# A gated-linear-attention and expert kernel: fill transfers spread over the loads, weights and an expert choice moved later in the order

## The chip, the cores and the metric

The kernel runs on one core of a Trainium2 chip. Its time is the device time of one execution in microseconds (us); smaller is better. Runs of one kernel are compared by their median. TensorE (PE) does the matmuls, VectorE (DVE), ScalarE (ACT) and GpSimd (POOL) the element work; SyncE (SP) issues most transfers. Each engine works through its own list of instructions in order.

## What is computed

A recurrence over 768 steps for 4 batches and 8 heads of width 48, and behind it a mixture of 16 experts in 4 groups. Each of the 3072 rows goes through the one expert that its two argmaxes pick:

```python
for t in range(S):
    state = alpha[:, :, t, :, None] * state + np.einsum('bhd,bhe->bhde', k[:, :, t], v[:, :, t])
    y[:, :, t] = np.einsum('bhd,bhde->bhe', q[:, :, t], state)
...
g_logits = x @ w_group
g_idx = np.argmax(g_logits, axis=1)
...
e_logits = xg @ w_expert[g]
e_idx = np.argmax(e_logits, axis=1)
...
h = np.maximum(xg[mask_e] @ w1[g, e], 0.0)
ye = h @ w2[g, e]
out[tok_idx] = combined[:, None] * ye
```

## The kernel before

**Chunks.** The recurrence is done in 24 chunks of 128 steps (six for each batch). For chunk n, DVE runs two scans over the decays (`rev`, line 445, and `forth`, line 456, with a small reciprocal `turn` between them), POOL multiplies keys and queries by their results (`key`, line 461, and `query`, line 465), and PE makes, in this order: the scores of chunk n+1 (`score`, line 477), its keys turned (`turn_k`, line 506), the rows of chunk n-1 with their logits (`row`, line 565), the gain of the state (`gain`, line 519), the outputs (`own_out`, line 543), and what the state adds (`from`, line 552). The scores are masked either by one DVE multiplication (line 486) or by an ACT copy (line 491) and a POOL select (line 494), once for each of the two halves of the heads; `BY_VECTOR[n]` says how many of chunk n's two halves DVE takes. The next chunk's scores go to the same PSUM banks, so `score` of n+1 waits for both masks of n. DVE adds the gain to the state (`grow`, line 528), ACT scales it in four pieces (`scale`, line 532) and copies the outputs (`copy`, line 558).

**Transfers.** A chunk's input is one array of 128 rows of 1925 numbers: decays, keys, queries, values. Chunks 0 and 1 come in pieces, the others whole. They land in six buffers (`in`), chunks 6 to 9 in the buffers of expert weights (`w`). All go through SP's list, with a few of the first ones through ACT's. Between them stand eight `fill` transfers, which write blank rows over the first 224 places of all 16 experts in the scratch tensor `slots_d` (line 777), and the weights of expert 0 (`w1`, `w2`). A fill needs the tile `blank`, which POOL makes (lines 243 and 244). Transfers signal on eight semaphores in turn, so at most eight are under way, and an issue waits until the one eight places earlier has landed.

**Experts.** After each batch (three smaller groups in the last batch) the experts of the rows are chosen, their places counted, and the rows scattered to `slots_d` by POOL (line 716). Expert 0 starts early with 96 rows. When three batches are counted, DVE chooses the expert with the most rows so far (`choose_ahead`, lines 328 to 338, step `ahead`), and SP loads its weights first (`w11`, `w21`). Then all experts run, with PE reading two weight matrices of 1.5 MB for each (line 271).

**The order** is not the one of the code. A planner, `Plan`, holds every step with its engine, an estimated duration and what it comes after; it walks through an imagined time, each engine taking the ready step with the longest way to the end, and the steps are emitted in the order that results. So a change of a dependency or of an estimate can move steps that the edit does not name. Tiles and semaphores see to correctness whatever the order.

## Time and profile before

| | us |
|---|---|
| median of 3 runs | 400.14 (399.95 to 401.26) |
| the profiled execution, whole | 400.82 |
| its span in the profile | 399.1 |
| first score of a chunk on PE | 8.54 |
| score of chunk 9, chunk 10 | 46.73, 60.06 |
| score of chunk 22, chunk 23 | 114.62, 121.33 |
| first matmul of the chosen expert | 144.11 |
| last matmul of the experts | about 388 |

The profile gives starts and durations in us from the start of the span. A note such as `[1.57 <-DMA w<-in_rows_dram]` behind a row says that the engine sat idle for so long just before, and what ended it. PEclk is the clock granted to PE, 1.00 being full speed.

### The profile page before, as it was taken

How to read it: one execution, taken by the hardware profiler on the slowest of the kernel's cores; microseconds unless marked ns; L12 is line 12 of the kernel's file. 1: busy time of each engine (PE TensorE's matmuls, PEld its weight loads, DVE VectorE, ACT ScalarE, POOL GpSimd, SP SyncE). 2: the span in 40 equal slices, each digit the busy share in tenths (PEclk: the TensorE clock that was granted, in tenths of full speed). 3: DMA queues.
4: the chain of work that ended last, by engine and by line, in shares of the span. 5: the costliest groups of instructions: out<-in, count | busy, mean ns of one | idle time of the engine just before them, and what ended most of it. 6: DMA issues, size and time to landing. Idle time of an engine off the chain costs nothing.

```text
span 399.1 us, 8686 instructions
## 1 busy us (share of the span) xinstructions
PE 379.2 (95%) x3381; PEld 362.3 (91%) x3381; DVE 160.8 (40%) x352; ACT 116.9 (29%) x307; POOL 199.0 (50%) x229
## 2 busy tenths in 40 slices
PE   7999669999999979999999999999999999999994
PEld 5888558888878979999999999999999999999993
DVE  6994578889987620202193021120220220220210
ACT  1576336675744211112121111211211211211120
POOL 4985847899964420234161442624534514424443
PEclk9999969999989989999999999999999999999998
DMA  8999992996657289776586765866868768666400
GB/s 306 399 395 379 400 414 83 369 339 227 224 199 270 108 255 256 290 213 214 190 266 236 247 208 192 278 243 214 235 252 265 224 243 284 208 266 237 179 21 31
DMA packets 30810, 98.35 MB, mean 246 GB/s; under 512 B 17989, under 2 KB 18371, under 8 KB 26416
## 3 DMA queue, kind: packets, MB, share of 16 engines
q1 hardware_dynamic: 24736, 86.88, 62.9%
q0 software_dynamic: 4832, 9.55, 7.1%
q10 hardware_dynamic: 1200, 1.36, 1.1%
q8 instruction: 27, 0.44, 0.5%
q14 instruction: 15, 0.12, 0.1%
HBM read 82.61 MB, written 15.60 MB: 246 GB/s over the span
## 4 chain that ended last, share of the span: by engine, by line
PE 83%; DVE 6%; DMA 5%; issue 2%; POOL 1%; ACT 0%; DVEq 0%; POOLq 0%
PE bank L271 61%; DMA in<-in_rows_dram 5%; PE bank L565 5%; PE zs L477 4%; PE zo L543 4%; PE zs L271 3%; PE bank L519 2%; PE zo L552 2%; DVE kd L445 2%; PE zo L506 2%; DVE cq L456 1%; POOL out_dram L1125 1%; DVE sm L486 1%; DVE cnt L323 1%; POOL in L465 0%
## 5 line engine op out<-in xcount | busy, mean ns | idle before, releaser
L1125 POOL DMA_INDIRECT out_dram<-yq,dst_q x101 | 98.1, 972 | 157.0 <-DVE yq L1121 109.5
L271 PE MATMUL bank<-hT,w 128*128 128x216 f32 (+14 forms) x720 | 120.8, 328 | 0.0
L271 PEld LDWEIGHTS bank<-hT,w 128*128 128x128 f32 x720 | 118.7, 190 | 0.0
L271 PE MATMUL bank<-xt_e,w 128*128 128x213 f32 (+14 forms) x720 | 117.4, 323 | 0.0
L271 PEld LDWEIGHTS bank<-xt_e,w 128*128 128x128 f32 x720 | 115.5, 190 | 0.0
L1142 DVE CAST dst_q<-xq 128x7 int32<-128x7 f32 (+1 forms) x14 | 2.4, 172 | 161.2 <-DMA out_dram<-yq,dst_q 161.2
L286 ACT ACTIVATE hT<-bank 128x432 f32<-128x432 f32 (+15 forms) x64 | 31.2, 488 | 98.7 <-PE bank L271 98.7
L302 ACT COPY yT<-bank 128x432 f32<-128x432 f32 (+29 forms) x30 | 12.1, 402 | 104.4 <-PE bank L271 104.4
L716 POOL DMA_INDIRECT slots_d<-xr,place x24 | 24.0, 1000 | 16.0 <-issue 8.5
L445 DVE TENSOR_TENSOR_SCAN kd<-in,starts 112x516 f32<-112x516 f32 x20 | 24.4, 1220 | 8.9 <-DMA in<-in_rows_dram 6.0
L565 PE MATMUL bank<-wr,yt 112*128 112x116 f32 x192 | 27.7, 290 | 0.2 <-ACT yt L558 0.2
L461 POOL TENSOR_TENSOR in<-in,kd 112x512 f32<-112x512 f32 x20 | 23.7, 1183 | 7.6 <-DVE kd L445 6.5
L477 PE MATMUL zs<-in 48*128 48x128 f32 x320 | 23.7, 284 | 3.0 <-POOL in L465 2.0
L465 POOL TENSOR_TENSOR in<-in,cq 112x512 f32<-112x512 f32 x20 | 23.6, 1181 | 5.4 <-PE bank L565 3.2
L565 PEld LDWEIGHTS bank<-wr,yt 112*128 112x128 f32 x192 | 25.0, 203 | 0.9 <-ACT yt L558 0.4
L477 PEld LDWEIGHTS zs<-in 48*128 48x128 f32 x320 | 19.7, 187 | 6.7 <-issue 3.3
L456 DVE TENSOR_TENSOR_SCAN cq<-in,starts 112x516 f32<-112x516 f32 x20 | 24.6, 1229 | 1.6
L1118 DVE STREAM_TRANSPOSE yq<-yT 128x672 f32<-128x672 f32 (+2 forms) x16 | 12.9, 807 | 27.5 <-ACT yT L302 27.5
L543 PE MATMUL zo<-sm,in 128*64 128x128 f32 (+1 forms) x320 | 23.1, 277 | 0.1
L532 ACT ACTIVATE state<-sums,kd 112x48 f32<-112x48 f32 x64 | 17.9, 330 | 10.6 <-DVE sums L528 10.6
L543 PEld LDWEIGHTS zo<-sm,in 128*48 128x48 f32 (+1 forms) x320 | 19.0, 132 | 0.7 <-POOL in L461 0.2
L558 ACT COPY yt<-zo 112x512 f32<-112x512 f32 x24 | 14.0, 585 | 15.6 <-PE zo L552 14.3
(152 smaller groups left out, 350.0 us busy)
## 6 DMA issues: line engine op xcount, KB each, us to landing
w<-in_w_dram SPq DMA_DIRECT2D x34, 1536.0 KB, 7.3
in<-in_rows_dram SPq DMA_DIRECT2D x18, 962.5 KB, 10.9
slots_d<-blank SPq DMA_DIRECT2D x8, 686.0 KB, 17.4
w<-in_rows_dram SPq DMA_DIRECT2D x4, 962.5 KB, 15.8
xq<-slots_d SPq DMA_DIRECT2D x28, 85.8 KB, 6.7
xq<-slots_d SPq DMA_DIRECT2D x28, 73.5 KB, 6.2
out_dram<-yq,dst_q POOLq DMA_INDIRECT x101, 5.5
in<-in_rows_dram ACTq DMA_DIRECT2D x2, 256.0 KB, 7.3
```

Of the source, the lines that this page charges most:

```text
L271: nc.tensor.matmul(z, lhsT=w, rhs=x, start=first, stop=last, skip_group_check=True)
L286: nc.scalar.activation(out=hT[:, f0:f0 + 2, 0:n], in_=z[:, 0:2 * n].rearrange("p (f t) -> p f t", f=2), func=AF.Relu)
L445: nc.vector.tensor_tensor_scan(out=flat(c.kd[:, p0:p1])[:, ::-1], data0=c.t[0:R, A1 * p1:A1 * p0:-1], data1=one_col.to_broadcast([R, A1 * ...
L456: nc.vector.tensor_tensor_scan(out=flat(c.cq[:, p0:p1]), data0=c.t[0:R, A1 * p0:A1 * p1], data1=starts[0:R, A1 * p0:A1 * p1], initial=1.0, ...
L461: nc.gpsimd.tensor_tensor(out=c.k[:, p0:p1], in0=c.k[:, p0:p1], in1=c.kd[:, p0:p1, 1:A1], op=ALU.mult)
L465: nc.gpsimd.tensor_tensor(out=c.q[:, p0:p1], in0=c.q[:, p0:p1], in1=c.cq[:, p0:p1, 1:A1], op=ALU.mult)
L477: nc.tensor.matmul(c.zs[i][:, p, :], lhsT=c.k[r, p, :], rhs=c.q[r, p, :], start=True, stop=True)
L532: nc.scalar.activation(out=c.st[:, p, 0:D], in_=chunks[c.n - 1].sums[:, p], func=AF.Copy, scale=c.kd[:, p, 0:1])
L543: nc.tensor.matmul(of(c.zo, p)[o], lhsT=c.v[:, h * D:h * D + o.stop - o.start], rhs=c.sm[:, i, p, :], start=(p < 2), stop=(c.bc == 0), ski ...
L565: nc.tensor.matmul(z[:, p * W:(p + 1) * W], lhsT=c.yt[:, p, :], rhs=wr[:, p, :], start=True, stop=True)
L716: sent = nc.gpsimd.indirect_dma_start(out=slots_by[t], out_offset=bass.IndirectOffsetOnAxis(ap=m["place"][:, c:c + 1], axis=0), in_=xr[:, ...
L1125: nc.gpsimd.indirect_dma_start(out=out_by.popleft().rearrange("n (j w) -> (n j) w", j=4), out_offset=bass.IndirectOffsetOnAxis(ap=dst[:, b ...
```

## The change

It has five parts, and the planner makes of them one new order.

1. The eight fills no longer stand in pairs before loads 8, 9, 10 and 11, but before loads 7, 8, 9 (two), 10, 11, 12 and 13. The first weights of expert 0 move from before load 15 to before load 16. The planner is also told that chunk 16 and later wait for the chunk six back, not ten.
2. ACT gets a one-column copy as its first step, which brings its table load to the front of its list.
3. Chunk 2 is sent in three pieces (decays, keys and queries, values); first pieces are dealt to SP and ACT in another way.
4. `choose_ahead` also comes after the places and the weights of its group, and has a smaller lead.
5. `BY_VECTOR` gives DVE 19 mask halves where it had 24.

```diff
+        def first_function():
+            nc.scalar.copy(out=zeros[:, 0:1], in_=nothing[:, 0:1])
...
-        BY_VECTOR = [0, 2, 1, 1, 1, 0, 1, 1, 0, 0, 1, 2, 0, 2, 0, 1, 0, 2, 2, 0, 1, 2, 2, 2]
+        BY_VECTOR = [0, 0, 0, 1, 1, 2, 1, 0, 1, 0, 1, 2, 0, 2, 1, 0, 0, 2, 2, 0, 1, 1, 0, 1]
...
         begin("decay0", False, 0, 0, AW)
-        begin("key_0", True, 0, AW, KQ)
-        begin("query_0", False, 0, KQ, VW)
-        begin("decay1", True, 1, 0, AW)
-        begin("key_1", False, 1, AW, KQ)
-        begin("query_1", True, 1, KQ, VW)
-        begin("load2", False, 2)
+        begin("key_0", False, 0, AW, KQ)
+        add("table", ACT, 1.5, first_function, row="act", after=["nothing"])
+        begin("query_0", True, 0, KQ, VW)
+        begin("decay1", False, 1, 0, AW)
+        begin("key_1", True, 1, AW, KQ)
+        begin("query_1", False, 1, KQ, VW)
+        begin("decay2", True, 2, 0, AW)
+        begin("key_2", False, 2, AW, VW)
         begin("value0", True, 0, VW, IW)
-        begin("load3", False, 3)
-        begin("value1", True, 1, VW, IW)
+        begin("value1", False, 1, VW, IW)
+        begin("load3", True, 3)
+        begin("value2", False, 2, VW, IW)
...
-        for i in range(FILLS):
-            before_load(8 + i // 2, ("fill", i))
-        for k, item in ((15, ("w1", 0)), (17, ("w2", 0))):
+        for i, k in enumerate((7, 8, 9, 9, 10, 11, 12, 13)):
+            before_load(k, ("fill", i))
+        for k, item in ((16, ("w1", 0)), (17, ("w2", 0))):
             before_load(k, item)
...
-                o = n - LATER
+                o = n - (LATER if n < LATER + NIN else NIN)
...
-            add("ahead", DVE, 1.1, choose_ahead, after=[f"count{AHEAD_T - 1}"], lead=20.0)
+            add("ahead", DVE, 1.1, choose_ahead,
+                after=[f"count{AHEAD_T - 1}", f"place{g}", made["weighed", g]], lead=8.0)
```

Three places of the new order matter below. PE's own order is the same as before.

**SP, the loads with the fills between them.** Before, from load 6 (`w_215`) on; `w` are chunks 6 to 9, the first `in` is chunk 10, and `slots_d<-blank` is a fill:

```order
L439 DMA w_215<-in_rows_dram 128x1925
L439 DMA w_248<-in_rows_dram 128x1925
L777 DMA slots_d<-blank 112x2x784 x2
L439 DMA w_354<-in_rows_dram 128x1925
L777 DMA slots_d<-blank 112x2x784 x2
L439 DMA w_452<-in_rows_dram 128x1925
L777 DMA slots_d<-blank 112x2x784 x2
L439 DMA in<-in_rows_dram 128x1925
L777 DMA slots_d<-blank 112x2x784 x2
L439 DMA in<-in_rows_dram 128x1925 x4
```

Now, from load 7 (`w_347`) on, one fill standing ahead of these rows:

```order
L442 DMA w_347<-in_rows_dram 128x1925
L780 DMA slots_d<-blank 112x2x784
L442 DMA w_415<-in_rows_dram 128x1925
L780 DMA slots_d<-blank 112x2x784 x2
L442 DMA w_510<-in_rows_dram 128x1925
L780 DMA slots_d<-blank 112x2x784
L442 DMA in<-in_rows_dram 128x1925
L780 DMA slots_d<-blank 112x2x784
L442 DMA in<-in_rows_dram 128x1925
L780 DMA slots_d<-blank 112x2x784
L442 DMA in<-in_rows_dram 128x1925
L780 DMA slots_d<-blank 112x2x784
```

Up to load 9 the same bytes stand ahead as before; ahead of load 10 stand five fills where six stood, ahead of load 11 six where eight stood.

**DVE, chunks 10 and 11.** Before, from the first scan of chunk 10 (`kd_668`) on; `kd_741` is the first scan of chunk 11, `sums_770` the `grow` of chunk 7:

```order
L445 SCALAR_TENSOR_TENSOR kd_668<-in_550,starts_114 112x516
L451 RECIPROCAL starts_114<-kd_668 112x4
L585 TENSOR_REDUCE lg_117<-lgp_121 128x120
L456 SCALAR_TENSOR_TENSOR cq_669<-in_550,starts_114 112x516
L445 SCALAR_TENSOR_TENSOR kd_741<-in_644,starts_114 112x516
L410 COPY starts_114<-desc_f_78 128x4
L411 COPY starts_114<-floor_f_79 128x1
L528 TENSOR_TENSOR sums_770<-state1_116,bank_747 112x192
```

Now, from the first scan of chunk 10 (`kd_678`); `sm_732` is a mask half of chunk 8, `sums_769` the `grow` of chunk 7:

```order
L448 SCALAR_TENSOR_TENSOR kd_678<-in_581,starts_114 112x516
L454 RECIPROCAL starts_114<-kd_678 112x4
L459 SCALAR_TENSOR_TENSOR cq_679<-in_581,starts_114 112x516
L588 TENSOR_REDUCE lg_117<-lgp_121 128x120
L489 TENSOR_TENSOR sm_732<-zs0_708,causal_68 128x512
L413 COPY starts_114<-desc_f_78 128x4
L414 COPY starts_114<-floor_f_79 128x1
L634 TENSOR_REDUCE starts_114<-lg_117 128x30
L531 TENSOR_TENSOR sums_769<-state1_116,bank_750 112x192
```

The `grow` of chunk 7 stood behind the first scan of chunk 11; now it stands ahead of it, behind the second scan of chunk 10, and a mask of chunk 8 has come to DVE. On ACT the copy of chunk 7's outputs, which stood behind the first `scale` piece that this `grow` feeds, stands behind the third.

**DVE, the choice of the expert.** Before, the last rows of `choose_ahead` (four more of its rows and the `own` of the group stand ahead), the group's weights and places, and the two masks of chunk 21:

```order
L336 TENSOR_TENSOR key_ahead_1702<-is_ahead_92,tile_f_76 128x15
L338 TENSOR_REDUCE ahead_i_93<-key_ahead_1702 128x1
L663 TENSOR_REDUCE sums_e_1730<-dl_1660 128x30
L665 SCALAR_TENSOR_TENSOR es_1732<-sums_e_1730,starts_114 128x24
L667 TENSOR_REDUCE starts_114<-es_1732 128x6
L668 SCALAR_TENSOR_TENSOR starts_114<-sums_e_1730,starts_114 128x6
L700 TENSOR_REDUCE place_1749<-own_1698 128x6
L670 RECIPROCAL xr_84<-starts_114 128x24
L486 TENSOR_TENSOR sm_1761<-zs0_1688,causal_68 128x512
L486 TENSOR_TENSOR sm_1761<-zs1_1689,causal_68 128x512
L451 RECIPROCAL starts_114<-kd_1671 112x4
```

Now, from the group's `own` to the first row of `choose_ahead` (`cnt18`):

```order
L696 TENSOR_TENSOR own_1702<-bank_1681,picked_81 128x96
L666 TENSOR_REDUCE sums_e_1707<-dl_1665 128x30
L668 SCALAR_TENSOR_TENSOR es_1713<-sums_e_1707,starts_114 128x24
L670 TENSOR_REDUCE starts_114<-es_1713 128x6
L671 SCALAR_TENSOR_TENSOR starts_114<-sums_e_1707,starts_114 128x6
L703 TENSOR_REDUCE place_1724<-own_1702 128x6
L673 RECIPROCAL xr_84<-starts_114 128x24
L489 TENSOR_TENSOR sm_1735<-zs0_1692,causal_68 128x512
L454 RECIPROCAL starts_114<-kd_1676 112x4
L459 SCALAR_TENSOR_TENSOR cq_1677<-in_1548,starts_114 112x516
L531 TENSOR_TENSOR sums_1762<-state0_115,bank_1739 112x192
L323 TENSOR_TENSOR cnt18_1774<-seen_83 128x16
```

The six rows of the choice have gone from ahead of the weights, places and masks to behind the second scan of chunk 23 and the `grow` of chunk 20. One of the two masks of chunk 21 has gone to ACT and POOL. ACT's register load of the chosen expert has gone from behind the turned keys of chunk 21 to behind the rows of chunk 22.

## The prediction

> **What bounds the kernel now.** I read the busy table first, then the stretches of the program, then PE's waits, then the chain that ended last.

> ```profile
> PE 379.2 (95%) x3381; PEld 362.3 (91%) x3381; DVE 160.8 (40%) x352; ACT 116.9 (29%) x307; POOL 199.0 (50%) x229
> ```

> PE is the bound over the whole span. Whether that holds in each stretch is seen from the window table (columns: window, its length, busy us and instructions of PE, PE weight load, DVE, ACT and POOL, then PEclk, DMA share, GB/s):

> ```profile
> 47.90:60.10 12.20, 6.48 (x71) 5.83 (x71) 8.40 (x19) 4.09 (x11) 6.70 (x9) 0.72 1.00 415
> 60.10:94.40 34.30, 34.30 (x553) 30.11 (x554) 29.74 (x57) 22.90 (x70) 29.50 (x32) 1.00 0.71 259
> ...
> 113.70:121.40 7.70, 6.74 (x82) 5.86 (x78) 6.04 (x15) 3.13 (x11) 6.00 (x6) 0.78 0.88 334
> ...
> 144.10:388.00 243.90, 243.89 (x1490) 243.69 (x1491) 50.06 (x117) 42.92 (x94) 94.84 (x98) 0.99 0.70 231
> ```

> From 144 to 388 us PE is never idle, and the change touches nothing there, so this part only starts earlier or later. From 60 to 94 PE is full too. Two stretches have holes and a lowered clock: 48 to 60, where DMA is at 100%, and 113.7 to 121.4. A gain can come from these two alone, and PE's waits name the first:

> ```profile
> PE zo L506 <- ACT yt L558: 5.7, 1, 5.7
> PE zs L477 <- DVE sm L486: 1.3, 1, 1.3
> ```

> The 5.7 us are one wait: PE had the scores of chunk 9 and then waited for ACT's copy of chunk 7's outputs. The chain of work shows what stood behind it, and that the matmuls after it ran slow; the last four rows are the same four steps of a chunk at 61 us:

> ```profile
> 53.62 1.01 PE zo L506 x4
> 54.63 1.71 PE bank L565 x8
> 56.34 0.91 PE bank L519 x13
> 57.25 1.67 PE zo L543 x16
> ...
> 61.23 0.53 PE zo L506 x4
> 61.76 0.90 PE bank L565 x8
> 62.66 0.54 PE bank L519 x13
> 63.19 0.95 PE zo L543 x15
> ```

> So the wait costs twice: its 5.7 us, and (1.01 + 1.71 + 0.91 + 1.67) - (0.53 + 0.90 + 0.54 + 0.95) = 2.4 us at half clock. The same kind of loss begins at the later place, where the clock falls (columns: window, length, PE busy us, PEclk, DMA share, GB/s):

> ```profile
> 116.50:117.00 0.50, 0.50 (x6) 0.63 0.98 418
> ```

> **Part 1, the fills: what frees PE at 53.6.** DVE in the time order, then ACT, then PE:

> ```profile
> 38.71 1.23 DVE L445 TENSOR_TENSOR_SCAN kd<-w,starts 112x516 f32<-112x516 f32 x1 [3.57 <-DMA w<-in_rows_dram]
> 44.94 1.23 DVE L445 TENSOR_TENSOR_SCAN kd<-in,starts 112x516 f32<-112x516 f32 x1 [2.87 <-ACT sm L491]
> 46.30 0.97 DVE L585 TENSOR_REDUCE lg<-lgp 128x120 f32<-128x480 f32 x1
> 47.16 1.24 DVE L456 TENSOR_TENSOR_SCAN cq<-in,starts 112x516 f32<-112x516 f32 x1
> 50.71 1.23 DVE L445 TENSOR_TENSOR_SCAN kd<-in,starts 112x516 f32<-112x516 f32 x1 [2.31 <-DMA in<-in_rows_dram]
> 52.38 0.34 DVE L528 TENSOR_TENSOR sums<-state,bank 112x192 f32<-112x192 f32 x1
> 52.65 0.28 DVE L631 TENSOR_REDUCE starts<-lg 128x30 f32<-128x120 f32 x1
> ```

> ```profile
> 52.76 0.34 ACT L532 ACTIVATE state<-sums,kd 112x48 f32<-112x48 f32 x1 [6.88 <-DVE sums L528]
> 53.00 0.56 ACT L558 COPY yt<-zo 112x512 f32<-112x512 f32 x1
> ```

> ```profile
> 46.73 1.16 PE L477 MATMUL zs<-w 48*128 48x128 f32 x16
> ```

> The three scans are those of chunks 9, 10 and 11, each waiting for its load (the ACT named at 44.94 had long been done, so I take that wait for the load as well). Chunk 11's load lands at 50.7; the `grow` of chunk 7 stands behind its scan, ACT's copy behind the `grow`, PE behind the copy. Between these landings lie 44.94 - 38.71 = 6.23 and 50.71 - 44.94 = 5.77 us, 6.0 on the average, for two fills and one load each. The sizes split that:

> ```profile
> in<-in_rows_dram SPq DMA_DIRECT2D x18, 962.5 KB, 10.9
> slots_d<-blank SPq DMA_DIRECT2D x8, 686.0 KB, 17.4
> ```

> A fill is 686 of 2 x 686 + 962.5 KB, so 1.76 us; a load 2.5 us. Load 9 has the same bytes ahead of it as before and should land at 38.7. Load 10 has one fill less: 44.94 - 1.76 = 43.2. Load 11 has two less: 50.71 - 3.52 = 47.2. Loads 12 and 13 follow with one fill each, 4.3 us apart, at 51.5 and 55.7.

> With the new order on DVE: scan of chunk 10 at 43.2; the two scans and the reciprocal take 2.6 (44.94 to the end of `forth` at 48.40 is 3.46, less the 0.86 from 46.30 to 47.16 in which the logits' sum stood between them); end 45.8. The logits' sum 0.97, a mask half 0.65 (half of 1.22, with a gap; the row stands below): 47.4. **Here PE gets the banks for the scores of chunk 9.** Before it had them at 46.73; with mask 7 off DVE the 1.3 us wait ahead of the scores of chunk 8 goes, so PE arrives at 45.4 and now waits 2.0 us. The two constants take 52.38 - (50.71 + 1.23) = 0.44, the maximum 0.28, the `grow` 0.34: 48.5. ACT then has three `scale` pieces at 0.24 (52.76 to 53.00) and the copy at 0.56 to do: 49.8. PE goes on at 49.9 in place of 53.62, a gain of **3.7 us**. Load 11's scan stands behind it and no longer holds anything up; the scans of chunks 12 and 13 are reached, by DVE's list at the same durations, at about 54 and 60 us, after their loads.

> The clock: the new hole is 2.0 us, then 1.1 of scores, then 1.4 us idle. I take it that the clock still falls and the 2.4 us are lost again, so they are no gain. The bounds are nothing lost (2.4 gained) and one more stretch as long (2.4 lost); the nearest row decides, that at 116.5, where the clock fell after much less idle time.

> **Part 4 and 5, the expert's choice and the masks at 110 us.** DVE, ACT, PE, then the chain:

> ```profile
> 109.68 2.07 DVE L323 TENSOR_TENSOR cnt<-seen 128x16 f32<-128x16 f32 x1 [0.24 <-ACT seen L689]
> 112.70 0.27 DVE L663 TENSOR_REDUCE sums_e<-dl 128x30 f32<-128x120 f32 x1
> 113.89 1.22 DVE L486 TENSOR_TENSOR sm<-zs,causal 128x512 f32<-128x512 f32 x2
> ```

> ```profile
> 113.36 0.48 ACT L570 COPY xr<-bank 128x384 f32<-128x384 f32 x1 [1.97 <-DVE es L665]
> ```

> ```profile
> 114.62 1.70 PE L477 MATMUL zs<-in 48*128 48x128 f32 x16 [0.87 <-issue]
> ```

> ```profile
> 116.94 1.71 PE bank L565 x8
> 118.66 0.91 PE bank L519 x13
> 119.57 1.24 PE zo L543 x16
> ```

> The choice holds DVE from 109.68 to 112.70, 3.0 us, ahead of the group's weights (1.2 us to 113.89) and both masks of chunk 21, for which the scores of chunk 22 wait. They ran 1.70 in place of 1.16 us after a wait of 0.87, so 1.4 us are lost. ACT's 1.97 us idle are its register load of the chosen expert. In the new order the weights begin when `own` is done, at 109.5, and the one mask on DVE ends at 111.3. The other goes to ACT, free there since the register load has moved away, and is copied by 112.0; POOL's select is in time for the outputs at 116.6. The scores can follow at 113.75 without a wait: **1.4 us**. Without the hole I expect no half clock: (1.71 + 0.91 + 1.24) - (0.90 + 0.54 + 0.95) = **1.5 us**. This second term has the bounds 0 (the clock falls all the same) and 1.5. The choice itself comes about 3.5 us later in the chunk order, and with it the weights of the chosen expert:

> ```profile
> w<-in_w_dram SPq DMA_DIRECT2D x34, 1536.0 KB, 7.3
> ```

> Two of them issued by about 117 on the old scale, even at twice 7.3 us, have landed by 132, and the first matmul that reads them starts at 144.1 (the window above): PE's last chunks and expert 0 hide it. If PE came to it earlier than they land, each us would count in full.

> Four mask halves of chunks 21 to 23 that now end on POOL stand between its scatters, each 0.64 us long:

> ```profile
> 18.00 0.64 POOL L494 TENSOR_SCALAR_AFFINE_SELECT sm<-sm 128x512 f32<-128x512 f32 x1
> ```

> POOL is busy 6.0 of the 7.7 us from 113.7 on; with 2.6 more it would have 8.6 to do, but its first scatter there waits for the weights, which come 3.0 us earlier. I cost this at nothing; the bound is 2 us lost.

> **Part 2 and 3, the start.** The table load and the pieces change when chunk 0 to 3 begin by a few tenths either way; the bound is 1.3 us, the length of the table load. Whatever it is, PE gives it back at the scores of chunk 9, which wait for load 10 and have 2.0 us of slack. I take nothing.

> **The sum.** 3.7 + 1.4 + 1.5 = 6.6 us. The profiled execution took 400.82 in all (399.1 of it span), 0.7 above the median; 400.82 - 6.6 = **394.2**.

> **The rivals.** *The clock stays up at 50 us.* The holes there are 2.0 and 1.4 us long, each shorter than the 5.7 that sank it; then the 2.4 us are gained as well, 391.8. Against it stands the clock row at 116.5, after 0.87 us and a short second wait. [...]

> *Only one of the two places gives.* If loads 10 and 11 do not land earlier, because fills run beside loads rather than in line, 3.7 goes: 397.9. If the hole at 113.7 is only moved to the next mask, 2.9 goes: 397.1. For it speaks that DMA is full until 60 us and all the bytes are still moved; against it the even spacing of the landings.

> *The change does not do what it says*: the order moves and PE waits as long elsewhere, 400.8.

> *Slower: the load stream runs dry at the first fill.* Fill 0 now stands in SP's list ahead of load 7, and cannot go before `blank` is made:

> ```profile
> 15.30 0.11 POOL L244 MEMSET blank<- 128x8 f32 x1
> ...
> 15.44 0.36 SPq L777 DMA_DIRECT2D slots_d<-blank  x1
> ```

> Two selects of chunk 1 (0.64 each, as above) now stand ahead of it on POOL, so 16.8 in place of 15.4. The 7.1 MB ahead of it last, at 415 GB/s, until 17 us plus the start, about 19.5. Every us past that delays loads 7 to 13 by one; to use up all 6.6 us of gain, POOL would have to be done only at 26 us. At 30 us the result would be 405.

> **How the numbers follow.** The forecast, both places with the clock falling at 50: 392.5 to 396.3, chance 0.60. Clock up: 0.12. One place only, 396.3 to 398.9: 0.17. Nothing: 0.05. Slower: 0.06. The range 391.0 to 397.9 takes in the forecast, the clock's rival, and most of the third. A measurement of this kernel can tell about 0.3% (1.2 us) from no change, so faster, by over 1.2 us, is 0.60 + 0.12 + 0.17 = 0.89; same 0.05; slower 0.06.

> **What would show it.** In the new profile the scan of chunk 10 at 43.2 and that of chunk 11 without a wait for its load; the turned keys of chunk 9 (PE, line 509) at 49.9; scores of chunk 10 at 56.4 (60.06 before); PEclk low between 50 and 55; no hole ahead of the scores of chunk 22 and PEclk 1.00 from 106 to 118; the chosen expert's first matmul at 137.5. A scan of chunk 10 at 44.9 would break the first term; a PE wait for a mask of chunk 21 or 22, or for a select, the second.

## The result, and the profile after

The changed kernel takes 388.95 us (median of 4 runs, 388.23 to 389.53), the kernel before 400.70 in the same set (399.95 to 402.12): ratio 0.970, with an interval of 0.967 to 0.974. The profiled execution took 389.36 us, with a span of 387.6. By the profiled executions the gain is 11.5 us, 1.7 times the forecast 6.6, and the time lies below the range of 391.0 to 397.9. Ratios and intervals, here and below, are of the executions that were not slowed; medians are of all.

PE's busy time falls by 4.7 us with the same 3381 matmuls: less of it runs at half clock (mean granted clock of the profiled executions 0.980 before, 0.997 now). The rest of the gain is holes. First the busy table of the changed kernel:

```profile
PE 374.5 (97%) x3381; PEld 357.6 (92%) x3381; DVE 157.9 (41%) x347; ACT 119.5 (31%) x313; POOL 202.5 (52%) x234
```

Then its window table for the two places of the prediction (same columns as there). PEclk is 1.00 in both, where it was 0.72 and 0.78:

```profile
47.90:60.10 12.20, 11.30 (x178) 9.74 (x174) 11.65 (x27) 8.60 (x26) 8.92 (x11) 1.00 0.99 408
113.70:121.40 7.70, 7.40 (x113) 6.39 (x112) 5.05 (x24) 3.99 (x13) 4.84 (x6) 1.00 0.98 367
```

DVE, ACT and PE of the changed kernel at the first place (start us, us, engine, line; the idle time before in brackets). DVE's rows are the first scan of chunk 10, a mask half of chunk 8, the `grow` of chunk 7 and the first scan of chunk 11; ACT's the copy of chunk 7; PE's the scores of chunk 9, the turned keys of chunk 9 and the scores of chunk 10:

```profile
42.64 1.23 DVE L448 TENSOR_TENSOR_SCAN kd<-in,starts 112x516 f32<-112x516 f32 x1 [1.77 <-ACT state L535]
46.22 0.68 DVE L489 TENSOR_TENSOR sm<-zs,causal 128x512 f32<-128x512 f32 x1
47.47 0.35 DVE L531 TENSOR_TENSOR sums<-state,bank 112x192 f32<-112x192 f32 x1
49.53 1.22 DVE L448 TENSOR_TENSOR_SCAN kd<-in,starts 112x516 f32<-112x516 f32 x1
```

```profile
48.54 0.56 ACT L561 COPY yt<-zo 112x512 f32<-112x512 f32 x1
```

```profile
47.00 0.69 PE L480 MATMUL zs<-w 48*128 48x128 f32 x7 [1.16 <-POOL in L468]
49.15 0.60 PE L509 MATMUL zo<-ident,w 112*128 112x112 f32 x4 [0.90 <-ACT yt L561]
53.28 0.49 PE L480 MATMUL zs<-in 48*128 48x128 f32 x3
```

The chain is the one forecast: scan 10, mask, `grow`, copy, PE; scan 11 no longer waits. The 5.73 us hole is now two, of 1.16 and 0.90. (The first is put down to POOL; I take it to be the wait for the mask half, which ended at 46.90, 0.10 us ahead.)

At the second place, DVE (the mask half of chunk 21, and one of the last rows of the choice) and PE (scores and turned keys of chunk 22) of the changed kernel:

```profile
103.78 0.63 DVE L489 TENSOR_TENSOR sm<-zs,causal 128x512 f32<-128x512 f32 x1
107.26 1.93 DVE L336 TENSOR_TENSOR key_ahead<-is_ahead,tile_f 128x15 f32<-128x15 f32 x1
```

```profile
106.90 1.16 PE L480 MATMUL zs<-in 48*128 48x128 f32 x16
108.00 0.60 PE L509 MATMUL zo<-ident,in 112*128 112x112 f32 x4
```

That mask is done 2.5 us before PE comes to the scores, which follow without a wait. The choice still holds DVE, but behind the mask.

The third place is not in the prediction. Window tables of before, then of the changed kernel, around the first matmul of the chosen expert (144.11 and 134.15):

```profile
140.60:144.00 3.40, 1.14 (x11) 0.97 (x9) 0.87 (x3) 0.24 (x1) 0.00 (x0) 0.99 0.81 162
144.00:147.40 3.40, 3.29 (x9) 3.14 (x10) 1.98 (x8) 0.00 (x0) 0.97 (x1) 0.51 0.94 289
147.40:150.80 3.40, 3.40 (x20) 3.40 (x20) 0.00 (x0) 0.97 (x2) 1.94 (x2) 1.00 1.00 394
```

```profile
130.70:134.10 3.40, 1.26 (x12) 1.10 (x10) 0.93 (x4) 0.56 (x2) 0.00 (x0) 1.00 0.73 150
134.10:137.50 3.40, 3.35 (x18) 3.38 (x19) 2.01 (x6) 0.53 (x1) 1.02 (x2) 1.00 1.00 301
```

PE waits here for the rows of the chosen expert in both, 2.37 and 2.19 us. Before, the clock then was half for 3.4 us: 9 matmuls where the same stretch has 18 now.

How the gain grows along PE's list, from the starts in PE's timeline:

| step on PE | before | after | earlier by | forecast |
|---|---|---|---|---|
| turned keys of chunk 9 | 53.62 | 49.15 | 4.47 | 3.7 |
| turned keys of chunk 10 | 61.16 | 54.38 | 6.78 | 3.7 |
| turned keys of chunk 21 | 110.17 | 103.40 | 6.77 | 3.7 |
| turned keys of chunk 22 | 116.25 | 108.00 | 8.25 | 5.1 |
| chosen expert's first matmul | 144.11 | 134.15 | 9.96 | 6.6 |
| end of the span | 399.1 | 387.6 | 11.5 | 6.6 |

### The profile page after: what moved, and what is told of

Its sections match the earlier page's. It is cut to its first block, busy times and chain, and to the rows that moved or that the text cites. A ratio compares the mean times of both kernels' runs of the same rounds, so it can differ in the third digit from the quotient of the medians.

```text
span 387.6 us, 8708 instructions
## 1 busy us (share of the span) xinstructions
PE 374.5 (97%) x3381; PEld 357.6 (92%) x3381; DVE 157.9 (41%) x347; ACT 119.5 (31%) x313; POOL 202.5 (52%) x234
## 4 chain that ended last, share of the span: by engine, by line
PE 91%; issue 2%; DVE 2%; DMA 1%; POOL 1%; ACT 1%; SPq 0%; POOLq 0%; DVEq 0%; ACTq 0%
PE bank L271 63%; PE zs L480 6%; PE zo L546 6%; PE bank L568 6%; PE zo L555 3%; PE zs L271 3%; PE bank L522 3%; PE zo L509 2%; DMA in<-in_rows_dram 1%; POOL out_dram L1132 1%; DVE kd L448 1%; ACT yt L561 0%; PE bank L745 0%; DVE cq L459 0%; POOL in L468 0%
## 5 line engine op out<-in xcount | busy, mean ns | idle before, releaser
L568 PE MATMUL bank<-wr,yt 112*128 112x116 f32 x192 | 26.1, 279 | 0.4 <-ACT yt L561 0.3
L568 PEld LDWEIGHTS bank<-wr,yt 112*128 112x128 f32 x192 | 23.3, 191 | 1.4 <-ACT yt L561 0.4
L480 PEld LDWEIGHTS zs<-in 48*128 48x128 f32 x320 | 19.5, 187 | 4.4 <-issue 1.7
L497 POOL TENSOR_SCALAR_AFFINE_SELECT sm<-sm 128x512 f32<-128x512 f32 x29 | 18.2, 641 | 3.3 <-ACT sm L494 3.2
L494 ACT COPY sm<-zs 128x512 f32<-128x512 f32 x29 | 16.7, 590 | 9.4 <-PE zs L480 9.4
## 6 DMA issues: line engine op xcount, KB each, us to landing
w<-in_w_dram SPq DMA_DIRECT2D x34, 1536.0 KB, 6.9
in<-in_rows_dram SPq DMA_DIRECT2D x16, 962.5 KB, 12.0
slots_d<-blank SPq DMA_DIRECT2D x8, 686.0 KB, 17.2
w<-in_rows_dram SPq DMA_DIRECT2D x4, 962.5 KB, 12.4
in<-in_rows_dram ACTq DMA_DIRECT2D x1, 962.5 KB
```

Source lines behind the costliest of these rows:

```text
L480: nc.tensor.matmul(c.zs[i][:, p, :], lhsT=c.k[r, p, :], rhs=c.q[r, p, :], start=True, stop=True)
L497: nc.gpsimd.affine_select(out=c.sm[:, i], in_=c.sm[:, i], pattern=[[0, HP], [1, P]], compare_op=ALU.is_ge, fill=0.0, base=0, channel_multi ...
L568: nc.tensor.matmul(z[:, p * W:(p + 1) * W], lhsT=c.yt[:, p, :], rhs=wr[:, p, :], start=True, stop=True)
```

## The experiments

They lay on four chips. On two of them (e1 to e4, e5 to e8) the kernel before took 411 us, and the traces of all kernels there have one or two more waits of some 2 to 4 us, on ACT or PE, between 120 and 140 us; of those runs I use the ratios and the traces up to 115 us. On the other two it took 401 (e9 to e16) and 399 us (e17, e18), near the 400.70 of the result. "Ratio" is to the kernel before on the same chip, with its 95% interval.

### Parts of the change, alone and left out

**Fills alone (e1, e16)** and **all but the fills (e2, e15)**: part 1 of the change (the fills, the first weights of expert 0, and the planner's rule for late loads), put into the kernel before, or taken out of the changed one.

```diff
-            before_load(8 + i // 2, ("fill", i))
+        for i, k in enumerate((7, 8, 9, 9, 10, 11, 12, 13)):
+            before_load(k, ("fill", i))
```

> The kernel before with the new places of the fills and of expert 0's weights alone. DVE's list around chunk 10 stays that of before: the grow of chunk 7 still stands behind the first scan of chunk 11. Theory 'loads': load 11 lands 3.5 us earlier, so that scan starts at 47.2 (50.71 before), the grow at 48.9 and the turned keys of chunk 9 at 50.1 (53.62), 3.5 us gained; with the clock falling as before the kernel is 3.5 us faster, 396.6 to 397; if the clock stays up there, 2.3 more, 394.5. Rival 'order': the loads land in another order but DVE's list holds PE all the same, under 0.5 us gained. The half clock at 116.6 and at 144 stays in both.

> The kernel before with the new fills alone. Theory 'loads': 3.9 us at the turned keys of chunk 10 as in its first trace, the half clock at 50 us, at 116 and at 144 stays: ratio 0.988 to 0.992. Rival: less than 1.5 us, since DVE's list still holds PE, ratio 0.996 or more.

> The changed kernel with the fills, expert 0's weights and the planner's rule for late loads as before. DVE's list around chunk 10 stays the new one, with the grow of chunk 7 ahead of the first scan of chunk 11. Theory 'loads': the scan of chunk 10 goes back from 42.64 to 44.9 and everything behind it with it, so the turned keys of chunk 9 stand at 51.4 in place of 49.15: 2.3 us slower than the changed kernel, about 391.3; the hole is then over 4 us and the clock falls, 2.3 us more, 393.5. Rival 'order': the new order alone has brought the gain at 50 us, the time stays within 0.5 us of the changed kernel, 389.

> The changed kernel with the old places of the fills, beside the masks alone. Theory: in this order the mask half of chunk 8, for which PE's scores of chunk 9 wait, stands behind the first scan of chunk 10, so it needs load 10 early; without the new fills PE waits 5 us there and the clock falls: 6 to 8 us slower than the changed kernel, ratio 0.986 to 0.992, no better than the masks alone. Rival: only the 2.3 us of load 10 are lost, ratio 0.977.

Measured: fills alone 404.23 (0.989, 0.981 to 0.996) and 396.27 us (0.989, 0.985 to 0.993); all but the fills 402.76 (0.987, 0.980 to 0.994) and 395.54 (0.987, 0.982 to 0.991). In e16 the `grow` of chunk 7 still stands behind the first scan of chunk 11 (46.46), but that scan starts 4.25 us earlier than the 50.71 of before. DVE (scan 11, `grow`) and PE (turned keys of chunk 9):

```profile
46.46 1.23 DVE L445 TENSOR_TENSOR_SCAN kd<-in,starts 112x516 f32<-112x516 f32 x1 [0.58 <-DMA in<-in_rows_dram]
48.13 0.34 DVE L528 TENSOR_TENSOR sums<-state,bank 112x192 f32<-112x192 f32 x1
```

```profile
49.37 0.32 PE L506 MATMUL zo<-ident,w 112*128 112x112 f32 x1 [1.87 <-ACT yt L558]
```

In e15 the new order is there without the early load. The mask of chunk 8 stands behind a scan that starts at 46.34, and PE waits for it. DVE (scan 10, mask) and PE (scores and turned keys of chunk 9):

```profile
46.34 1.23 DVE L448 TENSOR_TENSOR_SCAN kd<-in,starts 112x516 f32<-112x516 f32 x1 [4.69 <-DMA in<-in_rows_dram]
49.89 0.69 DVE L489 TENSOR_TENSOR sm<-zs,causal 128x512 f32<-128x512 f32 x1
```

```profile
50.69 0.58 PE L480 MATMUL zs<-w 48*128 48x128 f32 x5 [3.19 <-POOL in L468]
52.84 0.45 PE L509 MATMUL zo<-ident,w 112*128 112x112 f32 x1 [0.90 <-ACT yt L561]
```

So the loads do what was forecast, and the new order needs them: without them the turned keys stand at 52.84, near the 53.62 of before. 'Loads' holds in all four. Left out, the fills cost 6.2 us (e15 against the changed kernel on the same chip, 389.33 in e11), more than the 2.3 to 4.5 that e2 expected.

**Masks alone (e7, e14)** and **all but the masks (e18)**: the `BY_VECTOR` line, in or out.

> The kernel before with the new table of mask halves alone; fills, start and the choice as before. The table moves DVE's list: the grow of chunk 7 stands right behind the first scan of chunk 10, and of chunk 21 one mask half goes to ACT. Theory 'order': the turned keys of chunk 9 come at 48.5 in place of 53.6 though load 10 lands no earlier (scan of chunk 10 at 44.9 still), 4 to 7 us gained, 393.5 to 396.5 where before has 400.3. Rival 'loads': without the earlier loads the scores of chunk 10 wait for the second scan and the key product anyway, under 1.5 us gained.

> The kernel before with the new table of mask halves alone, beside the next two on one chip. Theory 'order': 4.5 to 6 us at the scores of chunk 10, as in its first trace (turned keys of chunk 10 at 56.5 in place of 61.2), the early choice still holds PE at 108 to 116: ratio 0.984 to 0.990. Rival: by itself it gives as much as the whole change, ratio 0.975 or less.

> The changed kernel with the old table of mask halves (24 on DVE): what is missing from the list of parts left out one at a time. Its order has the grow of chunk 7 behind five steps of the group's choice and ahead of the scan of chunk 11, and both halves of chunk 21 and 22 on DVE, with the choice behind them. Theory 'order': the copy of chunk 7 comes about 1.5 us later than in the changed kernel, and the scores of chunk 23 wait for the two masks of chunk 22 that stand behind the choice: 2 to 5 us slower than the changed kernel, ratio 0.975 to 0.984. Rival: fills and late choice alone do it, ratio 0.971 to 0.973.

Measured: masks alone 399.85 (0.974, 0.966 to 0.982) and 395.62 us (0.987, 0.984 to 0.991); all but the masks 390.47 (0.977, 0.973 to 0.982). Masks alone, the `grow` stands right behind scan 10, which is no earlier than before (46.28, against 44.94), and the turned keys of chunk 9 are early all the same. DVE, then PE of e14:

```profile
46.28 1.23 DVE L445 TENSOR_TENSOR_SCAN kd<-in,starts 112x516 f32<-112x516 f32 x1 [2.19 <-DMA in<-in_rows_dram]
47.43 0.33 DVE L528 TENSOR_TENSOR sums<-state,bank 112x192 f32<-112x192 f32 x1
```

```profile
48.87 0.45 PE L506 MATMUL zo<-ident,w 112*128 112x112 f32 x1 [1.54 <-ACT yt L558]
```

That is a second way to the same gain. (e14 has the ratio that was expected; e7, on its chip, gained more.) In company the table adds nothing that the trace of e18 shows: its turned keys of chunk 9 start at 48.31 and its chosen expert at 133.53, against 48.35 and 133.62 in the changed kernel (e11). There 'order' fell: the old table's list also has the `grow` ahead of scan 11 once the other parts are there, and the scores of chunk 23 did not wait. The ratio lies in the range that 'order' gave and is higher than that of e11, but it is from another chip; by the times alone this stays open.

**The late choice alone (e3)** and **all but it (e4, e12)**, part 4 in or out; **all but the new start (e10)**; and **the changed kernel itself (e5, e11)** beside them.

> The kernel before with the choice of the expert behind the group's weights and places, alone. Theory: the wait ahead of the scores of chunk 22 goes (1.4 us) and with it the half clock from 116.6 to 120.0 (1.5 us), so 2.9 us faster, 397.4 against 400.3, with everything up to 110 us as before. Rival: the wait moves to the next mask on DVE, 0 to 0.5 us gained.

> The changed kernel with the choice of the expert early again, alone. Theory: DVE is held 3.0 us ahead of the weights and the masks of chunk 21, and ACT by its register load, so the scores of chunk 22 wait 0.9 us or more and the clock falls behind it: 1.4 to 2.9 us slower, 390.4 to 391.9 where the changed kernel has 389. Rival: with one mask of chunk 21 on ACT and POOL the early choice costs nothing, within 0.5 us.

> The changed kernel with the early choice of the expert once more, beside the changed kernel on one chip, since the first time there was none beside it. Theory after the traces so far: with one mask half of chunk 21 on ACT and POOL the early choice no longer holds PE (5.17 us from the turned keys of chunk 21 to those of 22, against 5.16 in the changed kernel on another chip), so within 0.8 us of the changed kernel. Rival: the late choice is worth 1.4 us or more by itself.

> The changed kernel without the table load at the front and with the old pieces of chunks 0 to 3; fills, masks and the late choice stay new. Theory: PE gives the start back at the scores of chunk 9, so within 0.8 us of the changed kernel; the grow of chunk 7 stands one scan later in this order, which may cost up to 1 us. Rival: the start carries a part of the gain of its own, 1.5 us or more.

> The changed kernel once more, as the measure for the other runs of this set, since the four before it lay on a chip on which the kernel before took 405 to 415 us. If the gain is one of the program, the ratio to the kernel before is 0.965 to 0.974 here too, whatever the chip's own times; if it hangs on the chip, the ratio moves outside that.

> The changed kernel, as the measure for this set: ratio to the kernel before 0.962 to 0.974.

Measured: late choice alone 411.19 us (1.002, 0.994 to 1.009); all but it 398.08 (0.978, 0.972 to 0.985) and 392.12 (0.977, 0.974 to 0.981); all but the start 389.08 (0.972, 0.969 to 0.976); the changed kernel 396.07 (0.966, 0.958 to 0.974) and 389.33 (0.971, 0.968 to 0.974).

In e3 PE went from the turned keys of chunk 21 to those of 22 in 4.60 us, against 6.08 before: the wait ahead of the scores of chunk 22 is gone, as forecast. The time shows nothing of it (1.002): PE lost more behind 120 us in that execution, and no trace of the kernel before from that chip can be held beside it. So in the time the choice alone is not shown. My reading of e4, that the early choice costs nothing beside the new masks, fell with e12: 2.8 us slower than e11 on the same chip. DVE, POOL and PE of e12 (the first step of the choice; the two products of chunk 22 and 23; the scores of chunk 22):

```profile
103.07 2.22 DVE L323 TENSOR_TENSOR cnt<-seen 128x16 f32<-128x16 f32 x1 [0.24 <-ACT seen L692]
```

```profile
102.94 1.18 POOL L468 TENSOR_TENSOR in<-in,cq 112x512 f32<-112x512 f32 x1
104.08 1.17 POOL L464 TENSOR_TENSOR in<-in,kd 112x512 f32<-112x512 f32 x1
```

```profile
108.16 0.58 PE L480 MATMUL zs<-in 48*128 48x128 f32 x5 [1.03 <-issue]
```

A step on 128x16 numbers took 2.22 us, until POOL's two products were done (104.08 + 1.17 = 105.25). Behind it the mask of chunk 21 is late and PE waits 1.03 us; turned keys 21 to 22 take 5.78 us, against 4.60 in e11. That is 1.2 of the 2.8 us between the medians. The two profiled executions are 2.1 us apart; 1.0 of that comes from a wait at 85 us, where the two kernels have the same order, so I count it to the execution. Where the rest of the 2.8 us lies is not shown. The start is worth nothing, as forecast: e10 is within 0.3 us of e11.

### The clock by itself

**Constant matmuls in PE's holes of the kernel before (e6, e13)**, of the changed kernel (e8), and of its last hole alone (e17). Nothing reads what they write.

```diff
         for n in done:
+            if n in self.filler:
+                self.filler[n]()
             self.ops[n]["fn"]()
...
+        plan.filler = {"turn_k9": partial(warm, 36), "score22": partial(warm, 5), "end": partial(warm, 15)}
```

> The kernel before, with matmuls on a constant tile (nothing reads them) in three holes of PE: 36 ahead of the turned keys of chunk 9 (0.148 us each, 5.3 of the 5.7 us hole), 5 ahead of the scores of chunk 22, 15 behind the last step of expert 0. No wait is shortened by it. Theory 'clock': the three half-clock stretches at 51.6, 116.6 and 143.9 vanish, 2.4 + 1.5 + 1.6 = 5.5 us faster, 394.8 where the kernel before has 400.3. Rival 'the clock falls for another reason' (DMA at 100%, or the narrow matmuls): no gain, within 0.5 us of before.

> The kernel before with the constant matmuls in its three holes once more, since the first time the kernel before took 411 us on that chip, with waits of 2 to 3 us behind 120 us that are not in its profile here. On a chip where it takes 400 to 402, theory 'clock': low only once or not at all, mean clock 0.990 to 0.997 in place of 0.975 to 0.985, and 4 to 5.5 us faster (ratio 0.986 to 0.990). Rival: the last two low stretches come back behind other waits, only the 2.4 us at 54 us are gained (ratio 0.994).

> The changed kernel with the same constant matmuls in its three holes: 7 ahead of the scores of chunk 9, 5 ahead of the turned keys of chunk 9, 14 behind expert 0's last step. Theory: its clock does not fall in these holes, so nothing is to be won: within 0.5 us of the changed kernel on the same chip. Rival: in some executions the clock falls there all the same, and the mean gains up to 1.5 us.

> The changed kernel with 20 constant matmuls behind expert 0's last step (about 2.2 us, the length of its last hole of 2.1 to 2.5 us), nothing else. On the chip of the sets before, the changed kernel's mean clock was 0.992 or 0.993 in four of five executions and 0.997 in one, and its trace showed the low stretch right at this hole. Theory 'clock': the clock then stays up, 0.997 in most executions, 1 to 1.7 us faster than the changed kernel (389.3 there, so 387.6 to 388.3; ratio to before 0.967 to 0.969). Rival: the matmuls end later than the awaited rows in some executions, or the clock falls elsewhere: within 0.5 us, ratio 0.970 to 0.972.

Measured: e6 408.44 us (0.989, 0.982 to 0.996), e13 398.13 (0.994, 0.990 to 0.997), e8 397.78 (0.970, 0.963 to 0.978), e17 390.42 (0.980, 0.976 to 0.984). Windows of e13, at the three places:

```profile
47.90:60.10 12.20, 9.81 (x113) 8.42 (x111) 8.60 (x23) 5.12 (x16) 6.68 (x8) 0.86 0.99 414
113.70:121.40 7.70, 7.68 (x111) 6.49 (x111) 6.10 (x18) 3.53 (x12) 6.25 (x7) 1.00 0.94 361
140.60:147.40 6.80, 6.27 (x36) 6.00 (x35) 2.75 (x8) 1.06 (x2) 2.92 (x3) 1.00 0.97 324
```

The clock stays up at 116 and at 144 us, and no wait that PE had for another engine was shortened. At 50 us PE came a little earlier than before, the 36 matmuls lay from 46.8 to 50.9, 2.4 us of the hole were left behind them, and one low stretch out of two came back. This execution took 396.66 us, 4.2 less than the profiled one of before; the median gained 2.6, less than the 4 to 5.5 expected. The ratio is the one that the rival named (0.994), though it was the first low stretch that came back and not the last two. In e6 the clock stayed up at 50 us, and there PE went from the turned keys of chunk 9 to those of 10 in 5.22 us, against 7.54 before: 2.3 us, the 2.4 of the prediction. In the changed kernel the filler won nothing (e8 is 1.7 us slower than e5, within the intervals), and e17 is no better than the changed kernel by its ratio; its profiled execution has no low stretch, the others have a mean clock of 0.989 to 0.992, with no trace to say where. So the clock's price is shown for the kernel before; a filler in the changed kernel is no gain.

### A try to go further

**`grow` and mask earlier by hand (e9).** I put the remaining holes at 46 to 49 us down to DVE's order, so two steps were moved:

```diff
+        for n, ahead_of in (("mask0.8", "rev10.0"), ("grow7", "turn10.0")):
+            dve.remove(n)
+            dve.insert(dve.index(ahead_of), n)
```

> The changed kernel with two steps of DVE's list moved by hand: the mask half of chunk 8 ahead of the first scan of chunk 10, and the grow of chunk 7 right behind that scan. Theory: what is left of the hole at 46 to 49 us is DVE's order, not the loads. The scores of chunk 9 then start at 45.9 (47.00 before), the turned keys of chunk 9 at 47.0 (49.15), the scores of chunk 10 two us earlier: 1.5 to 2.1 us faster than the changed kernel, ratio to the kernel before lower by 0.004 to 0.005. Rival: PE then waits for the key and query products of chunk 10, or for later loads (that of chunk 16), and under 0.5 us is left.

Measured: 392.41 us (0.978, 0.975 to 0.981), 3.1 slower than e11 on the same chip. DVE (mask of chunk 8) and PE (turned keys of chunk 10) of e9:

```profile
45.84 0.69 DVE L506 TENSOR_TENSOR sm<-zs,causal 128x512 f32<-128x512 f32 x1 [3.76 <-POOL xr L256]
```

```profile
56.52 0.60 PE L526 MATMUL zo<-ident,in 112*128 112x112 f32 x4 [1.36 <-ACT yt L578]
```

The holes at 46 to 49 us are gone. But with the mask ahead of the scan DVE waits for PE, 3.76 us in this execution, in which PE ran 2.7 us behind e11 (turned keys of chunk 8 at 45.26 and 42.59). DVE's list from there to the `grow` of chunk 8 is 9.5 us without a gap, and PE waits one chunk later instead: 1.36 us, where e11 waits 0.90 at the turned keys of chunk 9. With 0.45 more at 73 us, ahead of scores that wait for a mask, that is 0.9 of the 3.1 us. This execution also lost 3.4 us to a low clock at 12 us, in code that is the changed kernel's own; whether the others did is not shown, and most of the loss has no place yet. No run beat the changed kernel clearly.

## Why the prediction was right, and where not

**Loads 10 and 11 earlier, PE at 49.9.** Right. Load 10 was there by 42.64 (43.2 forecast; in e11, where the scan's wait ends with the load itself, by 41.83), scan 11 ran without a wait, PE went on at 49.15. The term of 3.7 us measured 4.47, since the whole list stood 0.5 to 0.7 us sooner than I put it: the mask was done at 46.90 (47.4), the `grow` at 47.82 (48.5), the copy at 49.10 (49.8).

**"I take it that the clock still falls and the 2.4 us are lost again."** This step failed, and is the largest part of the miss. The clock stayed up, and turned keys 9 to 10 took 5.23 us where they took 7.54: 2.31 us gained that the sum had at nothing. It was my first rival, with a chance of 0.12. The two holes were 1.16 and 0.90 us long where I had 2.0 and 1.4. By the stretches of 3.41 us on which the clock's changes lay (last section), PE was idle for 1.13 us from 43.56 to 46.97 and for 0.93 from 46.97 to 50.38, where the kernel before had a stretch, 48.36 to 51.78, that was idle throughout. Between 47.90 and 60.10 PEclk is 0.72 before and in e15, with holes of 5.73 and 3.19 us; 0.86 in e16 and e14, with 1.87 and 1.54 us at the turned keys of chunk 9; and 1.00 in the changed kernel and in e9, with nothing longer than 1.16 and 1.36 us in the rows above. I had taken one row, at 116.5, for the rule; it fell there with 0.98 us, but at the scores of chunk 22 in e12 it stayed with 1.03.

**"From 144 to 388 us PE is never idle, and the change touches nothing there, so this part only starts earlier or later."** This failed too. The row said PEclk 0.99, and 0.01 of 243.9 us is room for a low stretch of 3.4 us; it stood at 144.0 to 147.4, behind a wait that ends where my window begins. From the chosen expert's first matmul to the end took 254.99 us before and 253.45 after: 1.54 us, missing from the sum. This part is luck and not the change: the wait is nearly as long as before (2.19 and 2.37 us), and whether a low stretch follows differs by execution. The four executions of the result, with a mean clock of 0.997 or 0.998, had none; e11 had it.

**The choice and the masks at 110 us, 1.4 + 1.5.** Right: 1.48 us by the turned keys of chunk 22 (8.25 - 6.77), and 1.71 more by the chosen expert (9.96 - 8.25). The scores of chunk 22 follow without a wait, PEclk is 1.00. By e3, e12 and e18 it is the choice that did it, not the masks. Most of the 3.0 us that the choice held DVE was one small step of 2.07 us that ended with a product of POOL (last section); a step like it is still there, 1.93 us at 107.26, where no mask that PE needs stands behind it.

**The start at nothing; no run dry at the first fill.** Right (e10; fill 0 was sent at 16.54, and PE lost no more behind it).

The sum of what the forecast missed: 0.77 (the loads, 4.47 for 3.7), 2.31 (the clock at 50 us), 0.28 (the choice with its half clock) and 1.54 (the chosen expert) make 4.9 us, which is 11.5 less 6.6. Of the 11.5 us some 5.5 (2.31 + 1.71 + 1.54) are the clock's, a price of waits more than a gain of its own. Over executions: before, on the chip of e9 to e16, had a mean clock of 0.975 to 0.985 in 26 executions, the changed kernel 0.992 to 0.997 in 5. A stretch of 3.41 us at half clock is 0.0043 of such a mean, and 0.997 is what an execution without any has (the profiled one), so these are about three to five stretches against none or one. In e11 the one came back, behind the same hole as in the kernel before:

```profile
129.80:133.80 4.00, 1.53 (x14) 1.40 (x13) 1.12 (x5) 0.56 (x2) 0.00 (x0) 1.00 0.69 148
133.80:137.20 3.40, 3.40 (x10) 3.19 (x10) 1.82 (x4) 0.00 (x0) 1.25 (x2) 0.50 0.94 299
```

The parts do not add up: alone 4.5 (fills, e16), 5.2 (masks, e14), and the choice not seen; left out, 6.2 (fills), 2.8 (choice), about 0 (start), and open for the masks (e18). Fills and masks both end the same wait of chunk 7's `grow` behind scan 11.

## What to carry to other kernels

Price a hole of a dense PE as its length plus the half clock that may follow it (here 5.73 us and 2.31 more at 50 us, 2.37 and 1.54 more at 144 us), and look for that also in the long "full" stretches, where a PEclk of 0.99 hides it (0.99 from 144.10 to 388.00, 0.51 from 144.00 to 147.40). Several orders of an engine's list can end the same wait: find what the waiting engine needs first, and see that it stands behind no transfer; leave-one-out runs tell what each part adds in company, parts alone do not. An engine whose list waits for the bottleneck itself can hand the hole on to the next stage (e9).

## What the runs showed of the hardware that I had not expected

**Small DVE steps were held until an instruction of POOL was done.** The first step of the choice took 0.17 us in the profiled run of the changed kernel, 2.07 before and 2.22 in e12, the latter two until POOL's products ended. In the changed kernel a later step took 1.93 (the row at 107.26 above), until a product of POOL ended at 109.15. In 19 of the 20 traces some step of the choice is held like this, and each time it ends 0.03 to 0.04 us behind an instruction of POOL (0.04 in the kernel before, in the changed kernel and in e12). In the kernel before, the first step ran from 109.68 to 111.75, and POOL's rows there are these, the second ending at 111.70:

```profile
109.41 1.17 POOL L465 TENSOR_TENSOR in<-in,cq 112x512 f32<-112x512 f32 x1
110.54 1.16 POOL L461 TENSOR_TENSOR in<-in,kd 112x512 f32<-112x512 f32 x1
```

The masks, the `grow` and the scans were not held: wholly beside the same products, in the traces of the two kernels, the masks took 0.63 to 0.69 us, the `grow` 0.33 to 0.36 and the scans 1.20 to 1.23; clear of the products they took 0.63 to 0.68, 0.33 to 0.36 and 1.20 to 1.23. In the program each of these has one operand in PSUM (for the scans `starts`); whether that is why is not shown.
